# Quarter-array attention at the start, and two moved steps in later passes, of an attention and mixture-of-experts kernel

## The chip, the cores and the metric

One core of a Trainium2 chip runs the kernel. Its engines work side by side: PE (TensorE, matmul; PEld is its weight load), DVE (VectorE), ACT (ScalarE), POOL (GpSimd) and SP (SyncE), which issues the DMAs here. They meet by semaphores. The metric is the device time of one execution in microseconds (us).

## The reference

The kernel computes an attention in chunks of 64 and feeds it to a mixture of four experts, all of which see every token:

```python
scores = scale * np.matmul(q_c, k_c.transpose(0, 1, 2, 4, 3))   # q, k, v: (8, 8, 576, 64), chunks of 64
scores = scores - np.max(scores, axis=-1, keepdims=True)
attn = np.exp(scores)
attn = attn / (np.sum(attn, axis=-1, keepdims=True) + 1e-09)
out = np.matmul(attn, v_c)
...
x = np.ascontiguousarray(attn_out.transpose(0, 2, 1, 3)).reshape(B * S, H * D)   # 4608 x 512
p = domain_probs / (domain_probs.sum(-1, keepdims=True) + 1e-09)
for e in range(E):                                   # 4 experts
    h = np.maximum(x @ w1[e], 0.0)                   # 512 x 1024
    out += p[:, e:e + 1] * (h @ w2[e])               # 1024 x 512
```

## The kernel before

**Tokens and passes.** The 4608 tokens are nine sub-blocks of 512. The first is worked on in eight plain passes (n = 0 to 7), the other eight in pairs: a pair takes eight passes (8 to 15, 16 to 23 and so on to 39), each over half an expert. A product of full precision is made of three: each operand is split in a hi part (a cast to fp32r, line L432 or L915, on ACT) and a lo part (the rest, L435 or L918, on POOL or DVE), and hi x hi, lo x hi and hi x lo are added up. For a pair a pass makes seven products of sums of blocks, not eight of blocks (Strassen's way); `t1` to `t4` and `b11` to `b22` are such sums of the hidden layer or its blocks, split by `sc.hi` and `sc.lo` for halves k = 0 and 1. L740 is the one line of all these matmuls: with xh or xl as weights they are the hidden layer, with hf the output layer.

**Order.** Each engine's instructions stand in the order in which the code is written; nothing reorders them. A later pass goes through a fixed list of products (`WOVEN`), and `add(at, i, f)` puts a step f ahead of its place i. A step that stands early on its engine is done early, and all that stands behind it on this engine waits for it.

**The startup.** Before pass 0 the attention of the first 512 tokens is made, in four tiles u of 128 tokens, beside the first hidden matmuls. Per tile: `start_scores` (L1115, 64x64 matmuls), `less_max` (DVE, L307 and L309), `a_exp` (ACT, L312), `start_weights` (sums and scale on DVE, L315 to L322), `start_transpose` (PE, L1121, and a copy by ACT, L1125), `start_values` (L1135), then the hi part (L432, ACT) and the lo part (L435, DVE) of the result, which the hidden matmuls read. A tile has two chunks c, whose operands lie in partitions 0 to 63 and 64 to 127. Scores and values of a chunk use the diagonal quarters of TensorE, rows c and columns c. The results lie in PSUM banks named A0, A1, B0, B1, C0, C1, and in psa, a tile of two banks that the attention of later tiles uses as well: there `quarters()` spreads scores (L161) and values (L208) over all four quarters, with the halves of v's second chunk swapped when it is loaded, `blocks(0)` of psa for scores and `blocks(1)` for values.

**Weights of later passes.** Their hi and lo parts are made once, stored in DRAM (`slots`, L581, L597) and read back in a ring (L635). `make_next` makes one unit on ACT and POOL (L577, L578) and appends its store to `kept`; `keep_made` issues the stores waiting in `kept`. `make_before` does the same for a unit of another pass (L592, L593, stores L597). All loads and stores stand in SP's queue in order, on eight DMA lanes in turn: an issue waits for the landing of the one eight before it.

Of the kernel before, what the change touches and what calls it, by code (L numbers as in the profile page):

```python
# [31 lines left out]
def chunk_attention_moe(ctx: ExitStack, tc: tile.TileContext, qk, v, v0, dp, w1, w2, out):  # L32
# [1069 lines left out]

    def start_v(t):
        nc.sync.dma_start(out=v0s[t // GT], in_=v0[:, t : t + GT])

    def start_scores(u):

        ps = psa[:, 1] if u == 2 else bank(("A0", "A1", None, "A1")[u])
        sc[u] = ps.rearrange("p (h s) -> p h s", s=C)
        for slot in range(2 * HG):  # L1110
            t, head = cell(u, slot)
            for c in range(2):
                rows = slice(c * C, (c + 1) * C)
                q, k = (qk0[t][rows, head // HG, x, head % HG] for x in range(2))
                nc.tensor.matmul(sc[u][rows, slot], lhsT=q, rhs=k, start=True, stop=True)  # L1115

    def start_transpose(u):

        w = (bank(("B0", "B1", "B1")[u]) if u < 3 else psa[:, 0]).rearrange("p (j s) -> p j s", s=P)
        for j in range(HG):  # L1120
            nc.tensor.transpose(  # L1121
                w[:, j], es[u][:, 2 * j : 2 * j + 2].rearrange("p h s -> p (h s)"), ident
            )
        pt[u] = hpool.tile([P, HG, P], F32, name=("s2", "s4")[u % 2])
        nc.scalar.copy(out=pt[u], in_=w)  # L1125

    def start_values(u):
        av[u] = bank(("B1", "B1", "B1", "A1")[u]).rearrange("p (j s) -> p j s", s=P)
        for j in range(HG):
            t, head = cell(u, 2 * j)  # L1130
            for c in range(2):
                for half in range(2):
                    rows = slice(half * C, (half + 1) * C)
                    cols = slice(c * C, (c + 1) * C)
                    nc.tensor.matmul(  # L1135
                        av[u][rows, j, cols], lhsT=v0s[t // GT][rows, t % GT, c, head // 2],
                        rhs=pt[u][rows, j, cols], start=True, stop=True,
                    )

# [5 lines left out]
    def start_x(u):  # L1145

        if u >= GT:
            return av[u], [part[:, :, u * P : (u + 1) * P] for part in xt["plain"]]
        return (
            av[u].rearrange("p (t j) s -> p t j s", t=GT),  # L1150
            [
                part[:, 2 * u : 2 * u + 2, first].rearrange("p j (t s) -> p t j s", t=GT)
                for part in xt["plain"]
            ],
        )

# [30 lines left out]
    def load_all():  # L1187
        for g in range(2):
            for t in range(GT):
                start_load(t, slice(g, g + 1))  # L1190
        start_v(0)
        w1_quad_load(0, 0, 0)
        w1_quad_load(0, 1, 0)
        start_load(2, slice(0, 2))
        w1_quad_load(0, 0, 1)
        w1_quad_load(0, 1, 1)
        start_load(3, slice(0, 2))
        w2_load(0, (0,))
        nc.sync.dma_start(out=pr, in_=dp)

    def start_weights(u):
        es[u] = att.tile([P, 2 * HG, C], F32, name=("e", "pt")[u % 2])

        scale(es[u], sc[u], inverse_sums(sc[u], psa[:, u != 2, : 2 * HG]))

    def startup(beside):
# [14 lines left out]
        start_values(0)  # L1221
        hi_part(*start_x(0))
        a_exp(sc[1])
        w1_split(1, 0, nc.gpsimd)
        lo_part(nc.vector, *start_x(0))
        start_weights(1)
# [9 lines left out]
        start_values(1)  # L1236
        hi_part(*start_x(1))
        w1_split(1, 1, nc.gpsimd)
        a_exp(sc[2])
        start_scores(3)  # L1240
        lo_part(nc.vector, *start_x(1))
        start_weights(2)
# [26 lines left out]
        start_values(2)  # L1269
        split(nc.vector, *start_x(2))  # L1270
        o[0].part((2, 3), slice(0, dm), False, True)
# [265 lines left out]
    def first_later_pass(n, held):  # L1537
# [5 lines left out]
        def put(i, name, k):  # L1543
# [43 lines left out]
    def later_pass(n, ahead, late, held):  # L1587
# [248 lines left out]
```

## Time and profile before

| what | value |
|---|---|
| three runs | 1470.07, 1470.26, 1470.32 us |
| median | 1470.26 us |
| the profiled execution | 1471.92 us, span 1469.8 us, granted TensorE clock 0.999 |
| busy in it: PE, PEld, DVE, ACT, POOL | 1459.9, 1200.5, 1079.4, 623.2, 975.0 us |
| DMA | 348.51 MB, mean 237 GB/s |

In a row of the timeline stand the start in the span, the duration, the engine, the line, the operation, out<-in with sizes, and in brackets how long the engine was idle before it and what ended that. A row with x32 is a burst of 32 records of one line. Matmuls overlap in the array, so a burst's duration is longer by a tail than its share of the chain of waits.

### The profile page before, as it was taken

How to read it: one execution, taken by the hardware profiler on the slowest of the kernel's cores; microseconds unless marked ns; L12 is line 12 of the kernel's file. 1: busy time of each engine (PE TensorE's matmuls, PEld its weight loads, DVE VectorE, ACT ScalarE, POOL GpSimd, SP SyncE). 2: the span in 40 equal slices, each digit the busy share in tenths (PEclk: the TensorE clock that was granted, in tenths of full speed). 3: DMA queues.
4: the chain of work that ended last, by engine and by line, in shares of the span. 5: the costliest groups of instructions: out<-in, count | busy, mean ns of one | idle time of the engine just before them, and what ended most of it. 6: DMA issues, size and time to landing. Idle time of an engine off the chain costs nothing.

```text
span 1469.8 us, 23359 instructions
## 1 busy us (share of the span) xinstructions
PE 1459.9 (99%) x8556; PEld 1200.5 (82%) x8556; DVE 1079.4 (73%) x1492; ACT 623.2 (42%) x1165; POOL 975.0 (66%) x728
## 2 busy tenths in 40 slices
PE   9999999999999999999999999999999999999998
PEld 7888887888887888888888888888888888888887
DVE  5567658888887886778767977777668866666666
ACT  4556635545454434444433435444334343233332
POOL 5778888788878785555557656555557655555555
PEclk9999999999999999999999999999999999999999
DMA  8798886878779779767566788776666786666665
GB/s 308 267 332 322 309 301 227 270 239 278 237 260 306 260 233 278 243 200 232 189 209 191 231 227 271 228 242 189 202 199 202 202 252 199 197 206 194 207 189 156
DMA packets 202882, 348.51 MB, mean 237 GB/s; under 512 B 70272, under 2 KB 116112, under 8 KB 202384
## 3 DMA queue, kind: packets, MB, share of 16 engines
q1 hardware_dynamic: 202768, 347.02, 73.8%
q8 instruction: 68, 1.11, 0.3%
q14 instruction: 46, 0.38, 0.1%
HBM read 275.59 MB, written 71.38 MB: 236 GB/s over the span
## 4 chain that ended last, share of the span: by engine, by line
PE 94%; DMA 2%; POOL 2%; DVE 1%; issue 0%; ACT 0%; SPq 0%; POOLq 0%; DVEq 0%; ACTq 0%
PE A L740 49%; PE C L740 27%; PE B L740 14%; POOL hf L918 1%; PE psa L208 1%; DMA wf<-w 1%; PE psa L161 1%; PE psa L263 1%; DMA out<-acc 1%; PE B L282 0%; POOL wf L578 0%; POOL hf L435 0%; DMA wf<-in_w 0%; DMA w_sums<-acc 0%; DMA pt<-w_sums 0%
## 5 line engine op out<-in xcount | busy, mean ns | idle before, releaser
L918 POOL TENSOR_TENSOR hf<-wraw,hf 128x512 fp32r<-128x512 f32 x384 | 507.9, 1341 | 225.0 <-ACT hf L915 223.8
L740 PE MATMUL A<-hf,wf 128*128 128x512 f32 x1536 | 391.5, 390 | 1.0 <-DMA wf<-w 1.0
L740 PE MATMUL A<-xh,wf 128*128 128x512 f32 (+1 forms) x1104 | 380.7, 388 | 0.2 <-POOL wf L578 0.2
L915 ACT CAST hf<-wraw 128x512 fp32r<-128x512 f32 x384 | 233.3, 622 | 290.7 <-DVE wraw L909 99.7
L740 PEld LDWEIGHTS A<-hf,wf 128*128 128x128 f32 x1536 | 286.5, 188 | 62.9 <-DVE acc L965 1.7
L740 PEld LDWEIGHTS A<-xh,wf 128*128 128x128 f32 x1104 | 206.7, 188 | 43.6 <-POOL wf L578 0.6
L803 ACT COPY s<-A 128x512 f32<-128x512 f32 x192 | 112.8, 587 | 290.9 <-PE A L740 290.6
L740 PE MATMUL A<-xl,wf 128*128 128x512 f32 (+1 forms) x552 | 213.7, 388 | 0.0
L965 DVE TENSOR_TENSOR acc<-A,acc 128x512 f32<-128x512 f32 x232 | 157.7, 680 | 64.8 <-PE A L740 64.5
L740 PE MATMUL C<-xh,wf 128*128 128x512 f32 (+1 forms) x600 | 203.6, 386 | 0.7 <-ACT xh L432 0.7
L740 PE MATMUL C<-hf,wf 128*128 128x512 f32 x768 | 195.0, 389 | 0.7 <-POOL hf L918 0.7
L740 PEld LDWEIGHTS C<-hf,wf 128*128 128x128 f32 x768 | 144.1, 188 | 31.0 <-POOL hf L918 1.1
L740 PEld LDWEIGHTS C<-xh,wf 128*128 128x128 f32 x600 | 111.5, 188 | 24.1 <-ACT xh L432 0.8
L909 POOL TENSOR_TENSOR wf<-wraw,wf 128x512 f32<-128x512 f32 x31 | 40.1, 1292 | 130.1 <-DVE wf L903 129.2
L740 PE MATMUL B<-xh,wf 128*128 128x512 f32 (+1 forms) x376 | 125.1, 383 | 0.0
L918 POOL TENSOR_TENSOR hf<-wf,hf 128x512 fp32r<-128x512 f32 x64 | 91.1, 1424 | 48.7 <-ACT hf L915 48.7
L740 PEld LDWEIGHTS A<-xl,wf 128*128 128x128 f32 x552 | 103.5, 188 | 21.1
L965 DVE TENSOR_TENSOR acc<-C,acc 128x512 f32<-128x512 f32 x120 | 82.6, 689 | 44.3 <-PE C L740 41.3
L740 PE MATMUL C<-xl,wf 128*128 128x512 f32 (+1 forms) x300 | 114.5, 385 | 0.0
L909 DVE TENSOR_TENSOR wraw<-wf,wraw 128x512 f32<-128x512 f32 x64 | 95.7, 1495 | 6.3 <-POOL hf L918 5.2
L740 PE MATMUL B<-hf,wf 128*128 128x512 f32 x384 | 97.9, 390 | 0.0
L909 POOL TENSOR_TENSOR wraw<-wraw 128x512 f32<-128x512 f32 x63 | 92.8, 1473 | 0.0
(224 smaller groups left out, 1969.3 us busy)
## 6 DMA issues: line engine op xcount, KB each, us to landing
wf<-w SPq DMA_DIRECT2D x402, 512.0 KB, 4.3
w<-wf SPq DMA_DIRECT2D x46, 512.0 KB, 5.2
w<-hf SPq DMA_DIRECT2D x28, 512.0 KB, 7.2
qk_in<-in_qk SPq DMA_DIRECT2D x24, 512.0 KB, 6.1
w<-hf SPq DMA_DIRECT2D x42, 256.0 KB, 5.2
wf<-in_w SPq DMA_DIRECT2D x19, 512.0 KB, 6.5
ws<-p_t SPq DMA_DIRECT2D x24, 256.0 KB, 4.1
xraw<-in_w SPq DMA_DIRECT2D x24, 256.0 KB, 4.7
```

The source lines that it names most:

```text
L161: nc.tensor.matmul(s["sc"][of_half(half), c, slot], lhsT=q, rhs=k, start=True, stop=True)
L208: nc.tensor.matmul(av[of_half(slot % 2), half, head // 2], lhsT=s["v"][of_half(half), head], rhs=s["pt"][of_half(half), c, slot], start=Tr ...
L263: nc.tensor.matmul(s["sc"][of_half(half), c, slot], lhsT=q, rhs=k, start=True, stop=True)
L740: nc.tensor.matmul(out, lhsT=lhs(k, a), rhs=rhs(k, b), start=first and i == 0, stop=last and i == len(parts) - 1, skip_group_check=not (fi ...
L803: nc.scalar.copy(out=t, in_=self.a)
L909: (eng or nc.vector).tensor_tensor(out=self.values[place, k], in0=self.values[a, k], in1=self.values[b, k], op=op)
L915: nc.scalar.copy(out=self.part(name, 0)[:, k], in_=self.values[name, k])
L918: (eng or nc.gpsimd).tensor_tensor(out=self.part(name, 1)[:, k], in0=self.values[name, k], in1=self.part(name, 0)[:, k].bitcast(F32), op=A ...
L965: nc.vector.tensor_tensor(out=acc[key], in0=src, in1=acc[key], op=ALU.add)
```

## The change

- Startup, scores and values: for tiles 0 to 2 the scores go over all four quarters into `blocks(0)` of psa (before: the diagonal, into A0, A1 and a bank of psa); tile 3 stays on the diagonal in A1. The values of all four tiles go over four quarters into `blocks(1)` of psa (before: B1, for tile 3 A1). The sums of the softmax lie in psa, in columns of `blocks(1)` (tile 3: of `blocks(0)`). The transposes go to B0 and B1.
- Startup, what follows from it: hi and lo of tiles 0 and 1 are two instructions each in place of one (`start_x_hi`, `start_x_lo`), one for each half of the result. v is loaded in three DMAs, chunk 0 and the two swapped halves of chunk 1, which for tiles 0 and 1 stand behind two weight loads.
- Pass 9: hi and lo of `t4`, k = 0, move from place 0 (put there by the list `late` of `first_later_pass`) to place 9, ahead of those of k = 1 at place 10.
- Pass 14: the three `keep_made` two places behind each `make_before` are left out; the stores go with the next `keep_made` in the code.

```diff
-    def start_v(t):
-        nc.sync.dma_start(out=v0s[t // GT], in_=v0[:, t : t + GT])
+    def start_v(t, chunks=(0, 1)):
+        to, of = v0s[t // GT], v0[:, t : t + GT]
+        if 0 in chunks:
+            nc.sync.dma_start(out=to[:, :, 0], in_=of[:, :, 0])
+        if 1 in chunks:
+            for half in range(2):
+                nc.sync.dma_start(out=to[of_half(half), :, 1], in_=of[of_half(1 - half), :, 1])
+
+    def start_blocks(u):
+        for pairs in ((0, 1), (2, 3)):
+            for p in range(2):
+                for c in range(2):
+                    for j in pairs:
+                        half, group = (j & 1, 2 * c + j // 2) if u < NT - 1 else (c, j)
+                        yield c, j, p, half, group, p ^ c
 
     def start_scores(u):
-        ps = psa[:, 1] if u == 2 else bank(("A0", "A1", None, "A1")[u])
-        sc[u] = ps.rearrange("p (h s) -> p h s", s=C)
-        for slot in range(2 * HG):
-            t, head = cell(u, slot)
-            for c in range(2):
-                rows = slice(c * C, (c + 1) * C)
-                q, k = (qk0[t][rows, head // HG, x, head % HG] for x in range(2))
-                nc.tensor.matmul(sc[u][rows, slot], lhsT=q, rhs=k, start=True, stop=True)
+        if u < NT - 1:
+            sc[u] = blocks(0)
+        else:
+            sc[u] = bank("A1").rearrange("p (c h s) -> p c h s", c=2, s=C)
+        for c, j, p, half, group, place in start_blocks(u):
+            t, head = cell(u, 2 * j + p)
+            q, k = (qk0[t][of_half(c), head // HG, x, head % HG] for x in range(2))
+            nc.tensor.matmul(
+                sc[u][of_half(half), group // 2, 2 * (group % 2) + place],
+                lhsT=q, rhs=k, start=True, stop=True,
+            )
...
     def start_values(u):
-        av[u] = bank(("B1", "B1", "B1", "A1")[u]).rearrange("p (j s) -> p j s", s=P)
...
+        av[u] = blocks(1)
+        for c, j, p, half, group, place in sorted(start_blocks(u), key=lambda block: block[1]):
+            t, head = cell(u, 2 * j + p)
+            nc.tensor.matmul(
+                av[u][of_half(p), c, j], lhsT=v0s[t // GT][of_half(place), t % GT, c, head // 2],
+                rhs=pt[u][of_half(place), group, of_half(half)], start=True, stop=True,
+            )
...
-        start_v(0)
+        start_v(0, (0,))
         w1_quad_load(0, 0, 0)
         w1_quad_load(0, 1, 0)
+        start_v(0, (1,))
         start_load(2, slice(0, 2))
...
-        scale(es[u], sc[u], inverse_sums(sc[u], psa[:, u != 2, : 2 * HG]))
+        i = 0 if u == NT - 1 else HG * C
+        z = psa[:, 0, i : i + 2 * HG].rearrange("p (c j) -> p c j", c=2)
+        scale(es[u], sc[u], inverse_sums(sc[u], z))
...
-            (0, lambda: sc.hi("t4", 0)), (0, lambda: sc.lo("t4", 0)), (7, lambda: sc.sum("t4", 1)),
+            (7, lambda: sc.sum("t4", 1)),
...
-        second_half(at, ahead[0], *((9, False, (1,)) if n == n_pass + 1 else ()))
+        second_half(at, ahead[0], *((9, False) if n == n_pass + 1 else ()))
...
         if n == 2 * n_pass - 2:
             for k, i in enumerate((11, 15, 18)):
                 add(at, i, lambda k=k: make_before(k))
-                add(at, i + 2, keep_made)
```

The places where the order changes, as the built programs have it. A row names line, operation, out<-in, and the semaphores that the instruction waits for, by engine or DMA lane. First PE in the startup, from scores(1) over values(0) to the first hidden matmuls; the rows before:

```order
L1115 MATMUL A_290<-xraw 64x64 [waits DMAHW2_49]
L1115 MATMUL A_290<-xraw 64x64 x7
L1115 MATMUL A_290<-xraw 64x64 [waits DMAHW3_49]
L1115 MATMUL A_290<-xraw 64x64 x7
L1135 MATMUL B_313<-s_288,qk_in 64x64 [waits DMAHW4_49,Activation_49]
L1135 MATMUL B_313<-s_288,qk_in 64x64 x15
L740 MATMUL C_342<-xh_236,wf_310 128x256 [waits Activation_49]
L740 MATMUL C_342<-xh_236,wf_310 128x256
```

and now:

```order
L1130 MATMUL psa<-xraw 64x64 [waits DMAHW2_49]
L1130 MATMUL psa<-xraw 64x64 x7
L1130 MATMUL psa<-xraw 64x64 [waits DMAHW3_49]
L1130 MATMUL psa<-xraw 64x64 x7
L1149 MATMUL psa<-s_289,qk_in 64x64 [waits DMAHW4_49,DVE_49,Activation_49]
L1149 MATMUL psa<-s_289,qk_in 64x64 [waits DMAHW0_49]
L1149 MATMUL psa<-s_289,qk_in 64x64
L1149 MATMUL psa<-s_289,qk_in 64x64 [waits DMAHW7_49]
L1149 MATMUL psa<-s_289,qk_in 64x64 x12
L740 MATMUL C_343<-xh_238,wf_310 128x256 [waits Activation_49]
L740 MATMUL C_343<-xh_238,wf_310 128x256
```

The scores write psa where they wrote A1; values(0) write psa where they wrote B1, and their first row waits for DVE too: for the subtraction L309 of tile 1. Values(1) do so for that of tile 2, values(2) for the reciprocal of tile 3. The other two new waits are those for the two halves of v's second chunk.

DVE at the same place, from less_max(1) to the scale of tile 1 (xl is the lo part of the attention's result); before:

```order
L307 TENSOR_REDUCE m_307<-A_290 128x8 [waits PE_49]
L309 TENSOR_TENSOR A_290<-A_290,m_307 128x512 [waits DVE_49]
L435 TENSOR_TENSOR xl_237<-B_313,xh_236 128x2x2x128 [waits Activation_49]
L315 TENSOR_REDUCE psa<-A_290 128x8 [waits Activation_49]
L316 TENSOR_SCALAR psa<-psa 128x8 [waits DVE_49]
L318 RECIPROCAL z_339<-psa 128x8 [waits DVE_49]
L322 TENSOR_TENSOR pt<-A_290,z_339 128x512 [waits DVE_49]
```

and now:

```order
L307 TENSOR_REDUCE m_307<-psa 128x8 [waits PE_49]
L309 TENSOR_TENSOR psa<-psa,m_307 128x2x256 [waits DVE_49]
L435 TENSOR_TENSOR xl_239<-psa,xh_238 128x2x2x64 [waits PE_49,Activation_49]
L435 TENSOR_TENSOR xl_239<-psa,xh_238 128x2x2x64
L315 TENSOR_REDUCE psa<-psa 128x8 [waits DVE_49]
L316 TENSOR_SCALAR psa<-psa 128x8 [waits DVE_49]
L318 RECIPROCAL z_340<-psa 128x8 [waits DVE_49]
L322 TENSOR_TENSOR pt<-psa,z_340 128x512 [waits DVE_49]
```

The lo part has become two instructions. Its wait on ACT was for the hi part; it is now for the exponential of tile 1, which stands behind the hi part on ACT, as that lies in the same banks.

POOL in pass 9 (hf_2683 before and hf_2795 now are t4; hf_2677 and hf_2680 are t1; L578 makes ring weights), before:

```order
L918 TENSOR_TENSOR hf_2616<-wraw,hf_2616 128x512
L918 TENSOR_TENSOR hf_2677<-wraw,hf_2677 128x512
L918 TENSOR_TENSOR hf_2683<-wraw,hf_2683 128x512
L918 TENSOR_TENSOR hf_2677<-wraw,hf_2677 128x512
L918 TENSOR_TENSOR hf_2707<-wraw,hf_2707 128x512 x2
L918 TENSOR_TENSOR hf_2723<-wf_2579,hf_2723 128x512
L578 TENSOR_TENSOR wf_2727<-xraw,wf_2727 128x2x256
L918 TENSOR_TENSOR hf_2723<-wf_2579,hf_2723 128x512
L578 TENSOR_TENSOR wf_2779<-xraw,wf_2779 128x2x256
L918 TENSOR_TENSOR hf_2683<-wraw,hf_2683 128x512
L578 TENSOR_TENSOR wf_2816<-xraw,wf_2816 128x2x256
```

and now:

```order
L918 TENSOR_TENSOR hf_2619<-wraw,hf_2619 128x512
L918 TENSOR_TENSOR hf_2680<-wraw,hf_2680 128x512 x2
L918 TENSOR_TENSOR hf_2707<-wraw,hf_2707 128x512 x2
L918 TENSOR_TENSOR hf_2723<-wf_2582,hf_2723 128x512
L578 TENSOR_TENSOR wf_2727<-xraw,wf_2727 128x2x256
L918 TENSOR_TENSOR hf_2723<-wf_2582,hf_2723 128x512
L578 TENSOR_TENSOR wf_2779<-xraw,wf_2779 128x2x256
L918 TENSOR_TENSOR hf_2795<-wraw,hf_2795 128x512 x2
L578 TENSOR_TENSOR wf_2819<-xraw,wf_2819 128x2x256
```

The first of the two pieces of t4 has moved down to the second, and what stood between the two (a piece of t1, three of other sums and blocks, two of L578) has moved up by one.

SP at the end of pass 14 (w_0_6_187 is the unit that `make_next` has made, w_0_0_195 and w_1_0_188 are loads for pass 15, w_1_1_203 and w_1_2_204 units of `make_before`), before:

```order
L597 DMA w_1_1_203<-pt 256x1x256 [waits DMAHW1_49,Pool_49]
L581 DMA w_0_6_187<-wf_5004 128x1024 [waits DMAHW2_49,Pool_49]
L635 DMA wf_5014<-w_0_0_195 128x1024 [waits DMAHW3_49,PE_49]
L635 DMA wf_5027<-w_1_0_188 128x1024 [waits DMAHW4_49,PE_49]
L597 DMA w_1_2_204<-xraw 256x1x256 [waits DMAHW5_49,Activation_49]
L597 DMA w_1_2_204<-v_in 256x1x256 [waits DMAHW6_49,Pool_49]
```

and now:

```order
L597 DMA w_1_1_203<-pt 256x1x256 [waits DMAHW5_49,Pool_49]
L635 DMA wf_5016<-w_0_0_195 128x1024 [waits DMAHW7_49,DMAHW6_49,PE_49]
L635 DMA wf_5029<-w_1_0_188 128x1024 [waits PE_49]
L581 DMA w_0_6_187<-wf_5007 128x1024 [waits DMAHW0_49,Pool_49]
L597 DMA w_1_2_204<-xraw 256x1x256 [waits DMAHW1_49,Activation_49]
L597 DMA w_1_2_204<-v_in 256x1x256 [waits DMAHW2_49,Pool_49]
```

The store of w_0_6 stands behind the two loads now. It waits for POOL; the loads wait for PE, which must have read the tiles that they fill.

More of the change, by code (lines that the diff above doesn't have):

```diff
@@ L1101, in start_load @@
         )
-    def start_v(t):
-        nc.sync.dma_start(out=v0s[t // GT], in_=v0[:, t : t + GT])
-    def start_scores(u):
-        ps = psa[:, 1] if u == 2 else bank(("A0", "A1", None, "A1")[u])
-        sc[u] = ps.rearrange("p (h s) -> p h s", s=C)
-        for slot in range(2 * HG):
-            t, head = cell(u, slot)
-            for c in range(2):
-                rows = slice(c * C, (c + 1) * C)
-                q, k = (qk0[t][rows, head // HG, x, head % HG] for x in range(2))
-                nc.tensor.matmul(sc[u][rows, slot], lhsT=q, rhs=k, start=True, stop=True)
+    def start_v(t, chunks=(0, 1)):
[12 more added lines that the diff above has]
+                        yield c, j, p, half, group, p ^ c
+    def start_scores(u):
+        if u < NT - 1:
[9 more added lines that the diff above has]
+            )
     def start_transpose(u):
-        w = (bank(("B0", "B1", "B1")[u]) if u < 3 else psa[:, 0]).rearrange("p (j s) -> p j s", s=P)
+        w = bank("B1" if u else "B0").rearrange("p (j s) -> p j s", s=P)
         for j in range(HG):
             nc.tensor.transpose(
-                w[:, j], es[u][:, 2 * j : 2 * j + 2].rearrange("p h s -> p (h s)"), ident
+                w[:, j], es[u][:, j // 2, 2 * (j % 2) : 2 * (j % 2) + 2].rearrange("p h s -> p (h s)"), ident
             )
@@ L1127, in start_values @@
     def start_values(u):
-        av[u] = bank(("B1", "B1", "B1", "A1")[u]).rearrange("p (j s) -> p j s", s=P)
[L1129 to L1138, printed above, removed]
+        av[u] = blocks(1)
[5 more added lines that the diff above has]
+            )
     first = slice(0, GT * P)
@@ L1145, in start_x, with start_x_hi, start_x_lo @@
     def start_x(u):
[L1147 to L1152, printed above, removed]
-                for part in xt["plain"]
-            ],
-        )
+        for t in range(GT) if u < GT else (u,):
+            j, k = (slice(2 * t, 2 * t + 2), slice(2 * u, 2 * u + 2)) if u < GT else (slice(0, HG),) * 2
+            yield av[u][:, :, j], [
+                part[:, k, t * P : (t + 1) * P].rearrange("p j (c s) -> p c j s", c=2)
+                for part in xt["plain"]
+            ]
+    def start_x_hi(u):
+        for x in start_x(u):
+            hi_part(*x)
+    def start_x_lo(u):
+        for x in start_x(u):
+            lo_part(nc.vector, *x)
     def start_hidden(u, fs, terms):
@@ L1201, in start_weights @@
     def start_weights(u):
-        es[u] = att.tile([P, 2 * HG, C], F32, name=("e", "pt")[u % 2])
-        scale(es[u], sc[u], inverse_sums(sc[u], psa[:, u != 2, : 2 * HG]))
+        es[u] = att.tile([P, 2, HG, C], F32, name=("e", "pt")[u % 2])
+        i = 0 if u == NT - 1 else HG * C
+        z = psa[:, 0, i : i + 2 * HG].rearrange("p (c j) -> p c j", c=2)
+        scale(es[u], sc[u], inverse_sums(sc[u], z))
     def startup(beside):
@@ L1221, in startup @@
         start_values(0)
-        hi_part(*start_x(0))
+        start_x_hi(0)
         a_exp(sc[1])
         w1_split(1, 0, nc.gpsimd)
-        lo_part(nc.vector, *start_x(0))
+        start_x_lo(0)
         start_weights(1)
@@ L1236, in startup @@
         start_values(1)
-        hi_part(*start_x(1))
+        start_x_hi(1)
         w1_split(1, 1, nc.gpsimd)
@@ L1240, in startup @@
         start_scores(3)
-        lo_part(nc.vector, *start_x(1))
+        start_x_lo(1)
         start_weights(2)
@@ L1269, in startup @@
         start_values(2)
-        split(nc.vector, *start_x(2))
+        start_x_hi(2)
+        start_x_lo(2)
         o[0].part((2, 3), slice(0, dm), False, True)
@@ L1275, in startup @@
         start_values(3)
-        split(nc.vector, *start_x(3))
+        start_x_hi(3)
+        start_x_lo(3)
         o[1].part((2, 3), slice(0, dm), False, True)
@@ L1699, in later_pass, with second_half @@
         return (sc, left), late, ()
-    def second_half(at, sc, t4=6, sum4=True, ks=range(2)):
+    def second_half(at, sc, t4=6, sum4=True):
         add(at, 0, lambda: sc.sum("t2", 1))
@@ L1708, in second_half @@
             add(at, 4, lambda: sc.sum("t4", 1, nc.gpsimd))
-        for k in ks:
+        for k in range(2):
             add(at, t4 + k, lambda k=k: sc.hi("t4", k), lambda k=k: sc.lo("t4", k))
```

## The prediction

> **What bounds the kernel.** I read the page first, then the waits of PE (TensorE), then the timeline of the places that the page cannot resolve: the first 33 us, and the ends of passes 9 and 14. Here is the page's busy time by engine, and all that PE waited for others from 100 us on (total, times, longest):
>
> ```profile
> PE 1459.9 (99%) x8556; PEld 1200.5 (82%) x8556; DVE 1079.4 (73%) x1492; ACT 623.2 (42%) x1165; POOL 975.0 (66%) x728
> PE A L740 <- DMA wf<-w: 1.0, 1, 1.0
> PE C L740 <- POOL hf L918: 0.7, 1, 0.7
> PE A L740 <- POOL wf L578: 0.2, 1, 0.2
> ```
>
> PE is busy for 1459.9 of 1469.8 us, so 9.9 us is all that hiding waits can bring. The edits of passes 9 and 14 aim at the three rows, 1.9 us together. And where PE has no idle time left, nothing swallows a delay: a microsecond lost in the startup is lost at the end.
>
> **Startup: what gets shorter.** Timeline (start, duration, engine, line, operation, out<-in; in brackets the idle time before and what ended it). L1115 are the scores, L1121 the transposes, L1135 the values; L307 and L309 less_max, L315 to L322 sums and scale, all on DVE (VectorE); L740 the hidden layer. The last row but two is a stretch of the table by windows, with DMA share and GB/s at its end:
>
> ```profile
> 3.86 1.97 PE L1115 MATMUL A<-xraw 64*64 64x64 f32 x32
> 10.04 0.63 PE L1121 MATMUL B<-ident,e 128*128 128x128 f32 x4 [1.39 <-DVE e L322]
> 10.60 1.15 PE L1115 MATMUL A<-xraw 64*64 64x64 f32 x32
> 11.58 1.10 PE L1135 MATMUL B<-s,qk_in 64*64 64x64 f32 x32
> 11.79 0.69 DVE L307 TENSOR_REDUCE m<-A 128x8 f32<-128x512 f32 x1 [1.90 <-PE A L1115]
> 12.52 0.70 DVE L309 TENSOR_TENSOR A<-A,m 128x512 f32<-128x512 f32 x1
> 13.36 1.22 PE L740 MATMUL C<-xh,wf 128*128 128x256 f32 x8 [0.69 <-ACT xh L432]
> 13.95 0.69 DVE L315 TENSOR_REDUCE psa<-A 128x8 f32<-128x512 f32 x1
> 14.42 0.64 PE L740 MATMUL C<-xl,wf 128*128 128x256 f32 x4
> 15.13 0.69 DVE L322 TENSOR_TENSOR pt<-A,z 128x512 f32<-128x512 f32 x1
> 16.35 0.60 PE L1121 MATMUL B<-ident,pt 128*128 128x128 f32 x4
> 17.87 1.10 PE L1135 MATMUL B<-s,qk_in 64*64 64x64 f32 x32
> 3.00:10.00 7.00, 5.65 (x45) 2.83 (x43) 3.16 (x6) 0.58 (x1) 0.00 (x0) 1.00 0.96 315
> 55.44 0.69 PE L208 MATMUL psa<-pt,v_in 64*64 64x64 f32 x32
> 55.96 0.70 PE L161 MATMUL psa<-qk_in 64*64 64x64 f32 x32
> ```
>
> The last two rows are values and scores as later passes do them, in four quarters: 0.70 us for 32 records, where the diagonal takes 1.15. So two scores and four values each save about 0.45. The first scores run slow (1.97); at 0.70/1.15 of that they take 1.20 and save 0.77. Softmax, transposes and the next scores hang on them: transposes(0) move from 10.04 to 9.27, and scores(1) run from 9.83 to 10.53. If nothing else changed, that would be 0.77 + 6 x 0.45, about 3.5 us.
>
> **Startup: the new waits.** Before, scores and values lay in different banks, and values(0) ran from 11.58, beside the softmax of tile 1. Now both lie in the two banks of psa, and in the instruction order values(u) carries a wait on DVE: for the subtraction (L309) of tile u+1 in the same banks. The lo part on DVE, likewise, now waits for the exponential of tile u+1 on ACT (ScalarE). Work that overlapped comes one after the other. Link by link, with these durations:
> - less_max(1) starts 0.04 behind scores(1), at 10.57, takes 0.69 and 0.70 and ends at 12.00. values(0) run from 12.12 to 12.81; before, they ended at 12.68. What scores(0) and scores(1) won is gone.
> - hi(0) becomes two casts of 128x256. The nearest row (ACT L747, next fence) has 0.66 for two; hidden(0) starts at 13.55 for 13.36: +0.19.
> - exp(1) (0.59, next fence) follows on ACT to 14.11, then lo(0), two pieces with 0.75 (DVE L748, next fence), from 14.15 to 14.90. The hidden matmuls that need it stood at 14.42: +0.53. Sums and scale of tile 1 took 13.95 to 15.82, 1.87; from 14.93 they end at 16.80, and transposes(1) start at 16.92 for 16.35: +0.57.
> - scores(2) run from 17.45 to 18.15, less_max(2) ends at 19.62, values(1) run from 19.74 to 20.43; before, they ended at 18.97: +1.46.
>
> The rows for tiles 2 and 3 (the one without a line's operation is from the chain of waits):
>
> ```profile
> 19.01 0.59 ACT L432 CAST xh<-B 128x512 fp32r<-128x512 f32 x1 [0.92 <-PE B L1135]
> 20.02 0.59 ACT L312 ACTIVATE psa<-psa 128x512 f32<-128x512 f32 x1
> 21.56 0.66 ACT L747 ACTIVATE hf<-C 128x256 fp32r<-128x256 f32 x2
> 21.82 0.69 DVE L322 TENSOR_TENSOR e<-psa,z 128x512 f32<-128x512 f32 x1
> 22.43 0.75 DVE L748 SCALAR_TENSOR_TENSOR hf<-C,hf 128x256 fp32r<-128x256 f32 x2
> 22.66 0.63 PE L1121 MATMUL B<-ident,e 128*128 128x128 f32 x4 [0.17 <-DVE e L322]
> 26.10 0.21 DVE L318 RECIPROCAL z<-psa 128x8 f32<-128x8 f32 x1
> 26.23 2.28 PE C L740 x9
> 29.17 0.68 DVE L435 TENSOR_TENSOR xl<-B,xh 128x512 fp32r<-128x512 f32 x1
> 29.67 1.15 PE L1135 MATMUL A<-s,ws 64*64 64x64 f32 x32
> ```
>
> - hi(1) starts at 20.45. exp(2) stood 1.01 behind the start of hi(1); with 0.07 for the split cast it runs from 21.53 to 22.12, lo(1) to 22.91, and 1.87 of sums and scale, with the gap ahead of them, to 24.81 for 22.51: +2.30. transposes(2) start at 24.95 for 22.66.
> - values(2) now wait for the reciprocal of tile 3, whose sums lie in psa as well. From the end of scale(2), 22.51, to that of this reciprocal, 26.31, DVE took 3.80; now 24.81 + 3.80 = 28.61. values(2) run from 28.73 to 29.35. Before, the next work on the chain began at 26.23: +3.1.
> - Behind them stands the same PE work as before, 26.23 to 29.67. So values(3) start at 32.79, take 0.70 for 1.15, and end at 33.5 for 30.82. Their wait for lo(2) ends earlier: DVE took 26.10 to 29.85 from reciprocal to lo(2), now 28.40 to 32.15.
>
> **Startup: +2.7 us.** Outer bounds: -3.5 if every new wait is hidden, +3.2 if values(3) win nothing. Each link is a row, so I stay with +2.7. The least sure is the wait of values(2): PE came from transposes(2) to them in 2.42, now by 27.37, and sits idle for 1.36; half of that hidden leaves +2.0. The three DMAs for v in place of one move the same bytes: with chunk 1 behind two weight loads, 2.1 MB have to land, at 315 GB/s and from about 3 us between 10 and 11, ahead of 12.1. Were that cover gone, values(0) would be late by the same amount.
>
> The Trainium skill, PSUM — Partial Sum Buffer, section "PSUM bank collisions raise a hardware error", has it that two engines are kept apart by bank and quadrant, not by address, which is how shared banks come to cost waits; a guard by address would leave the gains alone, the bound of -3.5. The instruction order has the guard; its price no run shows yet.
>
> **Pass 9.** PE and POOL (GpSimd) near its end:
>
> ```profile
> 228.93 10.35 POOL L918 TENSOR_TENSOR hf<-wraw,hf 128x512 fp32r<-128x512 f32 x7
> 236.64 0.74 PE L740 MATMUL C<-hf,wf 128*128 128x512 f32 x2 [0.70 <-POOL hf L918]
> 242.19 0.73 PE L740 MATMUL A<-xh,wf 128*128 128x512 f32 x2 [0.19 <-POOL wf L578]
> 245.05 1.29 POOL L918 TENSOR_TENSOR hf<-wraw,hf 128x512 fp32r<-128x512 f32 x1
> 247.31 1.63 PE L740 MATMUL A<-hf,wf 128*128 128x512 f32 x6
> ```
>
> POOL works without a gap, 10.35/7 = 1.48 us a piece, and PE waits for it twice, 0.70 and 0.19. One hi (ACT) and one lo (POOL) of t4 go from ahead of both waits to place 9: 1.3 to 1.5 us less on POOL ahead of them, more than 0.89. What is late next is t4 itself: its last lo ended at 246.34 and is used at 247.31, and with the moved piece in front it keeps that time, less the 0.89 that PE arrives earlier: 0.1 us of slack. Bounds: -0.89, and +0.5 if t4 is late by most of a piece. I take -0.9, as POOL has the same work in all.
>
> **Pass 14.** SP (the queue that issues DMAs), and from the chain of waits the load and PE's work behind it; the last row is the table by windows:
>
> ```profile
> 457.71 1.36 SPq L597 DMA_DIRECT2D w<-pt  x1
> 461.33 0.33 SPq L581 DMA_DIRECT2D w<-wf  x1
> 461.75 1.17 SPq L635 DMA_DIRECT2D wf<-w  x2
> 462.22 8.83 DMA wf<-w
> 471.18 3.01 PE A L740 x12
> 455.00:485.00 30.00, 28.97 (x128) 23.66 (x127) 21.50 (x26) 12.01 (x21) 25.68 (x19) 1.00 1.00 352
> ```
>
> SP stands from 459.07 to 461.33 at the store L581, whose data POOL had still to make, and two loads are queued behind it; the second lands at 471.05 and PE waits 1.03 for it. Now both stand ahead of the store and can go from 459.1. The DMA engines are full (share 1.00, 352 GB/s), so what counts is the bytes that go behind: 512 KB, or 1.49 us. The load lands at 469.6, ahead of 470.15. What is late next is the store, which no one reads in this pass. Bounds: 0, if something else holds the loads, and -1.03; I take -1.0.
>
> **Sum.** +2.7 - 0.9 - 1.0 = +0.8 us. The profiled execution took 1471.92 (span 1469.8), 1.66 above the median of 1470.26; I put the difference on the median: 1471.1.
>
> **Rivals.**
> - The gain is real: the new waits are hidden for the greater part. Startup between -3.5 and 0, at -1.7 a total of -3.6: 1466.7. For it speaks each shorter step; against it, that values(0) cannot start before 12.0 if they wait for a subtraction that needs scores(1). Chance 0.14.
> - Slower: PE loses its pace. The first scores took 1.97 for 32 records, the next 1.15. PE will now sit idle ahead of values(0), (1) and (2) for 1.6, 1.6 and 1.4 us. If one such gap brings the slow pace back, the hidden matmuls behind it, 3.0 us from 13.36 to 16.35, cost 0.71 more each: +2.1, in all +2.9, 1473.2; two gaps give 1475.3. One gap decides it. Against it: after 1.39 us of idling ahead of 10.04, scores(1) ran at 1.15. Chance 0.10.
> - The edits of passes 9 and 14 don't do what they say, startup as worked out: +2.7 and up to +0.5, 1473.0 to 1473.5. For it: the full DMA engines and t4's slack of 0.1. Chance 0.08.
>
> The Trainium skill, TensorE: Matmul & The Clock Gate, Part 1, says that the clock falls back after an idle window of about 3.4 us; by that rule none of these gaps is long enough, and the sum stays as it is.
>
> **How the numbers follow.** My own case has 0.68: from +2.0 - 1.9 to +3.2 - 0.4, 1470.3 to 1473.1. The range adds most of the gain's case below and half of the slow pace above: 1467.4 to 1473.9. A difference under 0.2%, 2.9 us, is about what a measurement cannot tell from none, so faster ends at 1467.3 and slower begins at 1473.2. Faster gets 0.10 of the gain's 0.14, and 0.04 for changes in the long passes that I don't see; slower gets 0.08 of the slow pace, 0.05 of the failed edits and 0.04 of my own case.
>
> **What would show it.** Scores(1) and all values at 0.70 us; PE idle ahead of values(0), (1) and (2) with DVE L309 or L318 as what ended it, 1.4 to 1.6 us each; values(3) ending near 33.5; no wait near 236.6 and 471.2. If values(0) start before 11.9, the wait is not what I take it for. If the twelve hidden matmuls after values(0) take over 2.5 us, PE lost its pace. A new wait of PE for t4 or for a later load would undo a pass's part.

## The result and the profile after

The changed kernel takes 1473.33 us (median of 21 runs, 1471.33 to 1474.13), the kernel before 1470.91 (21 runs, 1469.69 to 1473.58). The ratio is 1.0015, with a 95% interval of 1.0008 to 1.0021: slower by some 2.2 us, which is inside the 0.2% named above. The profiled execution of the changed kernel took 1473.44, its span is 1471.6.

How the loss and the gains lie along the span can be read from marks that both traces have: the first attention scores after the startup (L161), the last values before pass 9 (L208), the first scores behind pass 9, the last values before pass 14, and the last DVE copy. Timeline rows (start, duration, engine, line), before:

```profile
40.83 0.74 PE L161 MATMUL psa<-qk_in 64*64 64x64 f32 x32
160.90 0.69 PE L208 MATMUL psa<-pt,v_in 64*64 64x64 f32 x32
248.87 0.74 PE L161 MATMUL psa<-qk_in 64*64 64x64 f32 x32
447.47 0.69 PE L208 MATMUL psa<-pt,v_in 64*64 64x64 f32 x32
1465.86 0.42 DVE L1734 COPY s<-B 128x256 f32<-128x256 f32 x1 [0.53 <-PE B L1765]
```

and after:

```profile
45.66 0.74 PE L161 MATMUL psa<-qk_in 64*64 64x64 f32 x32
165.67 0.69 PE L208 MATMUL psa<-pt,v_in 64*64 64x64 f32 x32
252.22 0.74 PE L161 MATMUL psa<-qk_in 64*64 64x64 f32 x32
450.79 0.69 PE L208 MATMUL psa<-pt,v_in 64*64 64x64 f32 x32
1467.86 0.42 DVE L1756 COPY s<-B 128x256 f32<-128x256 f32 x1 [0.53 <-PE B L1787]
```

The shifts are +4.83, +4.77, +3.35, +3.32 and +2.00. So the startup lost 4.8 us, the stretch with pass 9 won 1.4, the one with pass 14 won 1.3, and between them the shift stayed within 0.06. From 36 us on the table of PE's waits has one row left, against four of before:

```profile
PE B L1787 <- DVE acc L1779: 0.3, 1, 0.3
```

The startup after (L1130 scores, L1139 transposes, L1149 values):

```profile
3.86 1.14 PE L1130 MATMUL psa<-xraw 64*64 64x64 f32 x32
9.22 0.63 PE L1139 MATMUL B<-ident,e 128*128 128x128 f32 x4 [1.90 <-DVE e L322]
9.78 0.69 PE L1130 MATMUL psa<-xraw 64*64 64x64 f32 x32
12.07 1.13 PE L1149 MATMUL psa<-s,qk_in 64*64 64x64 f32 x32 [1.59 <-issue]
13.96 2.07 PE L740 MATMUL C<-xh,wf 128*128 128x256 f32 x8 [0.76 <-ACT xh L432]
15.83 1.05 PE L740 MATMUL C<-xl,wf 128*128 128x256 f32 x4
19.04 0.60 PE L1139 MATMUL B<-ident,pt 128*128 128x128 f32 x4
21.91 0.69 PE L1149 MATMUL psa<-s,qk_in 64*64 64x64 f32 x32 [1.64 <-DVE psa L309]
30.90 0.69 PE L1149 MATMUL psa<-s,ws 64*64 64x64 f32 x32 [1.26 <-issue]
34.97 0.69 PE L1149 MATMUL psa<-s,ws 64*64 64x64 f32 x32
```

The scores became as short as expected, and PE waits ahead of values(0), (1) and (2) for 1.59, 1.64 and 1.26. But the rows from values(0) to 18.7 run slowly: 2.07 for eight hidden matmuls where before had 1.22, 1.13 for values(0) where values(1) take 0.69. The table by windows (length, busy of the engines, then PE's granted clock, DMA share, GB/s) shows why, after:

```profile
7.00:10.40 3.40, 1.50 (x38) 0.97 (x36) 1.77 (x4) 0.68 (x3) 0.00 (x0) 1.00 1.09 294
10.40:13.96 3.56, 1.21 (x39) 0.97 (x32) 1.39 (x2) 1.26 (x5) 1.26 (x1) 0.71 1.07 380
13.96:19.00 5.04, 5.04 (x24) 5.04 (x25) 2.52 (x6) 1.08 (x2) 1.28 (x1) 0.53 1.07 326
19.00:24.00 5.00, 3.36 (x106) 3.01 (x105) 1.39 (x2) 2.45 (x6) 1.36 (x2) 1.00 0.53 167
```

The two figures 0.71 and 0.53 are means: by the trace's clock records the granted clock is 0.50 from 11.92 to 18.75 us and 1.00 on either side. In the profile of before no such fall lies in the startup.

### The profile page after: what moved, and what is told of

Same layout as the page of the kernel before. It is cut to its first block, busy times and chain, and to the rows that moved or that the text cites. A ratio compares the mean times of both kernels' runs of the same rounds, so it can differ in the third digit from the quotient of the medians.

```text
span 1471.6 us, 23370 instructions
## 1 busy us (share of the span) xinstructions
PE 1458.2 (99%) x8556; PEld 1199.9 (82%) x8556; DVE 1078.6 (73%) x1494; ACT 623.2 (42%) x1167; POOL 975.6 (66%) x728
## 4 chain that ended last, share of the span: by engine, by line
PE 95%; POOL 2%; issue 1%; DVE 1%; ACT 1%; DMA 1%; POOLq 0%; SPq 0%; ACTq 0%
PE A L740 50%; PE C L740 27%; PE B L740 14%; POOL hf L435 1%; PE psa L208 1%; POOL wf L435 1%; PE psa L263 1%; PE psa L161 1%; PE B L282 0%; DMA w<-xl 0%; ACT hf L432 0%; PE psa L1149 0%; PE C L1204 0%; DMA w<-hf 0%; PE B L1139 0%
```

## The experiments

Each is compared with the kernel before on the same chip; its median there is given with it.

**The two parts of the change.** `passes` is the kernel before with the lines of passes 9 and 14 only:

```diff
-            (0, lambda: sc.hi("t4", 0)), (0, lambda: sc.lo("t4", 0)), (7, lambda: sc.sum("t4", 1)),
+            (7, lambda: sc.sum("t4", 1)),
-        second_half(at, ahead[0], *((9, False, (1,)) if n == n_pass + 1 else ()))
+        second_half(at, ahead[0], *((9, False) if n == n_pass + 1 else ()))
-                add(at, i + 2, keep_made)
```

> The kernel before with only the edits of passes 9 and 14. My theory: the three waits go, each costing more than its idle time, since the last matmul before it runs out its 0.39 us instead of handing over after 0.23 and the next pair starts slower; from the traces 1.42 in pass 9 and 1.33 in pass 14, 2.75 us together, so 1468.2 against 1470.9 for the kernel before. The rival (the 1.9 us of idle time that the waits' table shows is all): 1469.0. The waits' table from 100 us on should be empty but for the one at the end (0.3).

1469.55 for 1471.21, ratio 0.9988 (0.9979 to 0.9997): 1.7 us faster. In the profile all three waits are gone, and the last copy (DVE) stands at 1463.51, 2.35 earlier than in the profile of before. The median says less than this, and less than the 2.75 of my theory; it is nearest to the rival's 1.9. Why shows below.

`startup` is the other part: the changed kernel with these lines as they were.

> The kernel before with only the startup of the changed kernel. My theory: values(3) end 4.8 us later than before, 35.7 for 30.8, and nothing gives that back: 1475.7 against 1470.9. If parts of the 4.8 belong to the pace of PE and not to the waits, and the pace changes from run to run, the times spread by some 2 us. The rival (the startup is what the prediction's sum had, +2.7): 1473.6. The first later waits, 0.7, 0.2 and 1.0, are back.

1474.94 for 1471.21, ratio 1.0026 (1.0016 to 1.0036): 3.7 us slower, between the two theories. With the 1.7 of `passes` that gives +2.0, the 2.2 measured of both. So the parts add up within the noise, and the startup is where the change loses.

**Is it the clock?** `warm` gives PE more of the matmuls that only fill its idle time:

```diff
-WAITS = {"loads": 6, "softmax": 10}
+WAITS = {"loads": 6, "softmax": 17}
...
         start_scores(1)
+        keep_warm(6)
         less_max(sc[1])
```

> The changed kernel with more filler matmuls on PE (17 for 10 ahead of the first transposes, and 6 new ones between scores(1) and values(0)), which only fill its idle time. Theory A (part of the loss is PE's clock, which the profile grants at 0.53 to 0.71 from 10.4 to 19 us): granted clock 1.00 there, values(0) in 0.7 for 1.13, twelve hidden matmuls in 1.7 for 2.93, transposes(1) at about 17.3 for 19.04, and 1.7 us faster than the changed kernel: 1471.6 for 1473.3. Theory B (the slow stretch comes from something else, the DMA load at a share of 1.07 or the banks): the same 1473.3 and the same durations.

1471.92 for 1471.21, ratio 1.0004 (0.9995 to 1.0013), against 1.0015 of the changed kernel: by the medians, 1.4 to 1.7 us of the loss are the clock. Its windows:

```profile
10.40:14.00 3.60, 2.65 (x63) 1.50 (x56) 1.39 (x2) 1.74 (x5) 1.26 (x1) 1.00 1.07 365
14.00:19.00 5.00, 4.25 (x60) 3.74 (x59) 3.02 (x7) 1.98 (x4) 1.28 (x1) 1.00 1.08 335
```

and its timeline:

```profile
9.52 0.60 PE L1139 MATMUL B<-ident,e 128*128 128x128 f32 x4
12.34 0.69 PE L1149 MATMUL psa<-s,qk_in 64*64 64x64 f32 x32 [0.20 <-issue]
13.79 1.22 PE L740 MATMUL C<-xh,wf 128*128 128x256 f32 x8 [0.76 <-ACT xh L432]
17.21 0.60 PE L1139 MATMUL B<-ident,pt 128*128 128x128 f32 x4
20.07 0.70 PE L1149 MATMUL psa<-s,qk_in 64*64 64x64 f32 x32 [1.64 <-DVE psa L309]
25.32 0.63 PE L1139 MATMUL B<-ident,e 128*128 128x128 f32 x4 [0.31 <-DVE e L322]
29.07 0.70 PE L1149 MATMUL psa<-s,ws 64*64 64x64 f32 x32 [1.25 <-issue]
33.16 0.69 PE L1149 MATMUL psa<-s,ws 64*64 64x64 f32 x32
```

Clock 1.00, values(0) in 0.69, with the same DMA share and the same shared banks: theory B is out. Values(1) and (2) wait as they do after (1.64 and 1.25); ahead of values(0) the filler takes the place of the idle time, and they start no earlier. Transposes(1) stand 1.83 earlier than after, close to the 1.7 expected. The longer filler itself delays transposes(0) by 0.3.

**Are the waits those for the shared banks?** `v0banks` is the changed kernel with values(0) in banks of their own:

```diff
-        av[u] = blocks(1)
+        if u == 0:
+            av[u] = [bank(name)[:, : HG * C].rearrange("p (j k) -> p j k", k=C) for name in ("A1", "B1")]
+            to = lambda c: av[u][c]
+        else:
+            av[u] = blocks(1)
+            to = lambda c: av[u][:, c]
...
-                av[u][of_half(p), c, j], lhsT=v0s[t // GT][of_half(place), t % GT, c, head // 2],
+                to(c)[of_half(p), j], lhsT=v0s[t // GT][of_half(place), t % GT, c, head // 2],
...
```

> The changed kernel, but values(0) go to two banks of their own (A1 for chunk 0, B1 for chunk 1), still in four quarters; hi and lo of tile 0 are made by chunk. Theory A (values(0) wait for the subtraction because they share psa's banks with scores(1)): they start when the copied transposes and v are there, 10.5 to 11.2 for 12.07, lo(0) no longer waits for the exponential of tile 1, and with one gap less PE keeps its clock: transposes(1) at about 16.0 for 19.04, 2.5 to 3 us faster than the changed kernel, 1470.6. values(1) still sit idle for 1.6. Theory B (it is v's second chunk that comes late, or the four quarters themselves): values(0) start at 12.0 as before and the time stays at 1473.3.

```profile
10.31 0.33 PE L1154 MATMUL A<-s,qk_in 64*64 64x64 f32 x2
11.04 0.37 PE L1154 MATMUL B<-s,qk_in 64*64 64x64 f32 x1 [0.40 <-DMA qk_in<-in_v]
17.98 0.60 PE L1139 MATMUL B<-ident,pt 128*128 128x128 f32 x4
20.84 0.69 PE L1154 MATMUL psa<-s,qk_in 64*64 64x64 f32 x32 [1.64 <-DVE psa L309]
```

Values(0) start at 10.31 for 12.07, so it was the shared banks that held them, though the profile of the changed kernel puts that wait down to "issue". They then wait 0.40 for v's second chunk: it lands at about 11.0, which the 12.0 of the changed kernel covers. Values(1), still in psa, sit idle for 1.64 as before. What I had not expected: the clock fell in this profile too (0.57 from 10.4 to 14 us), and transposes(1) came at 17.98, not 16.0. The median is 1471.41 for 1471.12, ratio 1.0000 (0.9991 to 1.0009); the runs lie from 1469.95 to 1473.46, five of eleven below 1470.7. The eight runs whose granted clock is 0.999 or 1.000 have a median of 1470.58, the 1470.6 that theory A expected with the clock held.

`z3` is `warm` with the sums of tile 3 in SBUF:

```diff
+        if u == NT - 1:
+            z = small.tile([P, 2, HG], F32, name="zsum")
...
```

> The changed kernel with the added filler (so that the clock holds), and with the softmax sums of tile 3 in SBUF instead of psa. Theory A (values(2) wait for the reciprocal of tile 3 because its sums lie in their bank): the idle time of 1.25 us ahead of values(2) at 29.07 goes; values(3) then wait for lo(2) on DVE at about 32.2 and give some of it back: 0.8 to 1.2 us faster than with the filler alone, 1470.9 for 1471.9. Theory B (something else ends that wait): values(2) still start at 29.07.

```profile
27.38 0.69 PE L1149 MATMUL psa<-s,ws 64*64 64x64 f32 x32
32.75 0.69 PE L1149 MATMUL psa<-s,ws 64*64 64x64 f32 x32 [1.06 <-DVE xl L435]
31.93 0.68 DVE L435 TENSOR_TENSOR xl<-psa,xh 128x512 fp32r<-128x512 f32 x1
```

The wait ahead of values(2) is gone, so it was the reciprocal's. But values(3) wait 1.06 for lo(2) instead, and lo(2) stands on DVE behind softmax and normalising. From transposes(0) (9.15 here, 9.52 in `warm`) to values(3) it is 23.60 against 23.64. The time, 1471.33 for 1471.12, ratio 1.0001 (0.9993 to 1.0010), can't be told from `warm`. Expected were 0.8 to 1.2 us: a wait removed at one place came back at the next, with DVE as the bound.

**What lowers the clock?** `gap5` is `passes` with less filler ahead of the first transposes:

```diff
-WAITS = {"loads": 6, "softmax": 10}
+WAITS = {"loads": 6, "softmax": 5}
```

> The kernel with only the edits of passes 9 and 14 (1469.55), and 5 filler matmuls for 10 ahead of the first transposes, so that PE sits idle for some 2.8 us there instead of 1.4 to 1.6; all that follows is as before. Theory A (the clock falls with the share of time that PE works in a stretch of some us, so that two gaps of 1.9 and 1.6 did it in the changed kernel, and this one does it too): granted clock under 1.00 somewhere from 10 to 16 us, hidden(0) slower, 1 to 2 us longer. Theory B (only an idle stretch of about 3.4 us, the figure of the Trainium skill, TensorE: Matmul & The Clock Gate, Part 1, lowers it): granted clock 1.00 in all stretches, 1469.6.

The transposes of `gap5` with their idle time in the timeline:

```profile
9.27 0.63 PE L1121 MATMUL B<-ident,e 128*128 128x128 f32 x4 [3.03 <-DVE e L322]
```

and its windows:

```profile
7.00:10.40 3.40, 1.13 (x23) 1.00 (x25) 1.77 (x4) 0.68 (x2) 0.00 (x0) 1.00 1.03 364
10.40:14.00 3.60, 2.92 (x55) 2.73 (x52) 2.03 (x4) 1.89 (x5) 1.27 (x1) 0.56 1.07 383
14.00:19.00 5.00, 5.00 (x35) 4.83 (x36) 1.73 (x5) 0.48 (x2) 1.27 (x1) 0.63 1.03 405
```

An idle stretch of 3.03, with none of the change's banks and waits, lowers the clock to a mean of 0.56. The times spread from 1468.96 to 1473.99 (median 1471.14 for 1471.12): in some executions it falls and in some it doesn't. And it can fall in the startup of before. The run of `pass9` (below) that was profiled shows it, behind an idle stretch of 1.95 alone; timeline, then windows:

```profile
9.25 0.63 PE L1121 MATMUL B<-ident,e 128*128 128x128 f32 x4 [1.95 <-DVE e L322]
```

```profile
10.40:14.00 3.60, 2.92 (x55) 2.73 (x52) 2.03 (x4) 1.87 (x5) 1.26 (x1) 0.55 1.07 383
```

This execution took 1472.07; the other nine of the same kernel took 1469.35 to 1469.79. So the fall cost about 2.4 us there. In the profile of `pass14` an idle stretch of 1.94 at the same place, 0.8 later in time, left the clock at 1.00:

```profile
10.04 0.63 PE L1121 MATMUL B<-ident,e 128*128 128x128 f32 x4 [1.94 <-DVE e L322]
```

Length alone does not decide, then. The clock records kept in the traces show what does go with the fall. They begin where PE first gets its full clock, and that time differs from execution to execution. It shows in the length of scores(0), here in `pass9`, with the same diagonal matmuls that took 1.97 in the profile of before:

```profile
3.86 1.18 PE L1115 MATMUL A<-xraw 64*64 64x64 f32 x32
```

Count stretches of 3.41 us from that time on. In each of the five traces with a fall, the clock falls at the end of the second stretch and stays at 0.50 for the next two, 6.83 us. The busy share is that of PE in this second stretch, by the table by windows:

| trace | full clock from, us | idle time ahead of transposes(0) | second stretch, us | PE busy in it | clock at its end |
|---|---|---|---|---|---|
| after | 5.10 | 1.90 | 8.51 to 11.92 | 0.37 | falls |
| `startup` | 4.43 | 1.97 | 7.84 to 11.26 | 0.37 | falls |
| `v0banks` | 4.05 | 1.96 | 7.46 to 10.88 | 0.46 | falls |
| `gap5` | 4.00 | 3.03 | 7.42 to 10.83 | 0.46 | falls |
| `pass9` | 3.96 | 1.95 | 7.38 to 10.79 | 0.45 | falls |
| `best` (below) | 3.99 | 1.96 | 7.41 to 10.82 | 0.54 | holds |
| `pass14` (below) | 5.73 | 1.94 | 9.14 to 12.56 | 0.74 | holds |
| `passes` | 6.52 | 1.59 | 9.93 to 13.34 | 0.77 | holds |
| before | 6.92 | 1.39 | 10.33 to 13.74 | 0.80 | holds |

In the 13 traces of this case, counted in this way up to 1450 us, these five are the only stretches in which PE was busy for less than half of the time; the next lowest has 0.52, and the clock held. So it is the share of work in a stretch of 3.41 us that goes with the fall, and where the stretches lie differs between executions of one kernel. This is read off the traces afterwards; no run sets the place of the stretches. The Trainium skill, TensorE: Matmul & The Clock Gate, Part 1, has the clock fall after an idle window of about 3.4 us and speaks of a free-running window; the traces agree with such a window and not with the need for 3.4 us of rest: a window in which PE worked for 0.37 to 0.46 of the time was enough.

The timed runs show the same. A fall of 6.83 us to half the clock takes 0.0023 off the mean granted clock, which each run lists. Of the 21 runs of the changed kernel 13 have 0.997 or 0.998 (median 1473.44) and eight have 0.999 or 1.000 (median 1472.47); of the kernel before, on the three chips of the experiments, 7 of 83 have 0.997; of `gap5` 7 of 10 have 0.998 or less; of `warm`, `z3` and the three faster kernels below none of 48. So the fall is in most executions of the changed kernel, and without it that kernel is still slower than the kernel before. The two groups of its runs lie only 1.0 apart. One reason is in the traces: the falls came with an early full clock (3.96 to 5.10 us), which can shorten scores(0), as in `pass9`.

**The passes one by one.** `pass9` and `pass14` are the kernel before with the one or the other of the two edits.

> The kernel before with the edit of pass 9 alone. Theory (each of the two waits costs its idle time and the tail of the matmul ahead of it, and the first pair behind it is slow): the attention of pass 10 begins 1.4 us earlier, 247.5 for 248.87, though the waits' table loses only 0.9; the wait for the load at the end of pass 14 stays. 1.0 to 1.4 us faster than the kernel before. The rival (t4 comes late in return): a new wait of PE near 246, and 0.4 us or less.

> The kernel before with the edit of pass 14 alone. Theory: SP issues both loads at about 459 instead of 461.8 and 462.2, the wait of 1.0 us for the load goes, 1.0 to 1.3 us faster than the kernel before; the two waits of pass 9 stay. The rival (other loads of the full DMA engines come later in return): a new wait for a load between 470 and 490, no gain.

`pass9`: 1469.62 for 1470.83, ratio 0.9992 (0.9983 to 1.0001, which just reaches none), 1.2 us; no wait for t4 appears. `pass14`: 1471.03 for 1470.83, ratio 1.0002 (0.9993 to 1.0011), no gain that can be measured (the interval reaches from 1.0 us faster to 1.6 slower), although in its profile SP issues both loads 2.3 us earlier and no wait for a load is left:

```profile
459.50 1.83 SPq L635 DMA_DIRECT2D wf<-w  x2
```

The table of waits shows what there was to win. The same wait, unedited, in the profiles of `pass9` and then of `startup`:

```profile
PE A L740 <- DMA wf<-w: 0.4, 1, 0.4
```

```profile
PE A L740 <- DMA wf<-w: 0.7, 2, 0.5
```

It is 0.4 and 0.7 there, where the profile of before has 1.0: the DMA engines are full at this place (share 1.00 in the prediction's windows), and the wait varies from profile to profile. The profiled execution of before took 1471.92, 1.0 above the median of its 21 runs. A wait read from that one execution can be worth less in the median. The traces speak for some gain: from the last values before pass 14 to the last copy it is 1016.89 to 1017.46 us in the ten profiles with the edit and 1017.73 to 1018.39 in the three without. Whether it is worth nothing or a whole microsecond the timed runs don't settle.

**The gain without the waits.** `scores4` is `passes`, and of the startup only the scores in four quarters, with the values where they were and v in one DMA. Against the lines of the changed kernel:

```diff
-                        yield c, j, p, half, group, p ^ c
+                        yield c, j, p, half, group, p
...
-        av[u] = blocks(1)
+        av[u] = bank(("B1", "B1", "B1", "A1")[u]).rearrange("p (j s) -> p j s", s=P)
...
-                av[u][of_half(p), c, j], lhsT=v0s[t // GT][of_half(place), t % GT, c, head // 2],
+                av[u][of_half(p), j, of_half(c)], lhsT=v0s[t // GT][of_half(p), t % GT, c, head // 2],
```

> The edits of passes 9 and 14, and of the startup's change only the scores: in four quarters, in psa, while values stay on the diagonal in B1 and A1 with v as it was. No bank is shared, so no new wait stands in the order. Theory A (the loss is the shared banks' waits): scores(0) save 0.8, scores(1) and (2) 0.45 each, so the startup ends 1.3 to 1.7 us earlier than before, and with 2.75 of the passes the time is 1466.6. Theory B (four quarters in the startup lose by themselves, as PE gets more idle time and its clock drops): granted clock under 1.00 between 10 and 19 us and a startup that is no shorter, 1468.2 or more.

1468.74 for 1471.21, ratio 0.9982 (0.9973 to 0.9991). The first L161 stands at 39.79 for 40.83: the startup is 1.04 shorter, less than the 1.3 to 1.7 expected, with the clock at 1.00. Against `passes`, measured beside it, the median is 0.8 shorter. No shared bank, no wait, a gain.

`best` adds the values of tiles 2 and 3 in four quarters in psa (with `p ^ c` for these tiles, and their second chunk of v swapped) and the sums of tile 3 in SBUF; `best2` also moves `norm_probs()` behind lo(2).

> The version with scores in four quarters and values(0), (1) on the diagonal (1468.74), and now values(2) and (3) in four quarters in psa, where no scores lie any more at that time, with the sums of tile 3 in SBUF. Theory A (four quarters gain their 0.45 us wherever no shared bank puts a wait on the path): values(2) in 0.70 for 1.20 without a wait, values(3) the same but up to 0.3 late for lo(2): 0.6 to 0.9 us faster, 1468.0. Theory B (PE isn't the bound there, DVE's chain is): values(3) end no earlier, 1468.7.

> The version with scores and the last two tiles' values in four quarters (1467.45), with the normalising of the probabilities on DVE moved behind lo(2). Theory A (DVE's order ahead of lo(2), 2.3 us of that normalising, makes the 0.80 us that values(3) wait): the wait goes, values(3) start at 27.8 for 28.56, 0.7 us faster, 1466.7. Theory B (the first use of the probabilities, the scaling of the output block on DVE, then comes late and holds a bank): values(3) start early, but PE waits later; the time stays at 1467.4.

`best`: 1467.45 for 1471.12, ratio 0.9972 (0.9960 to 0.9983). `best2`: 1467.18 for 1470.83, ratio 0.9975 (0.9966 to 0.9985). The timeline has the values of tiles 2 and 3 in `best`:

```profile
23.64 0.69 PE L1152 MATMUL psa<-s,ws 64*64 64x64 f32 x32
28.56 0.69 PE L1152 MATMUL psa<-s,ws 64*64 64x64 f32 x32 [0.80 <-DVE xl L435]
```

and those of tile 3 with the first wait behind them in `best2`:

```profile
28.07 0.70 PE L1152 MATMUL psa<-s,ws 64*64 64x64 f32 x32
30.87 0.39 PE L740 MATMUL B<-xl,wf 128*128 128x256 f32 x1 [0.41 <-DVE xl L435]
```

In `best` values(3) wait for lo(2). In `best2` that wait is gone, and PE waits 0.41 for lo(3) instead. Both versions beat the kernel before by some 3.7 us and can't be told apart. That is theory B of `best2`, with another wait than the one it named.

## Why the prediction was right, and where it was off

- **The total.** +0.8 was forecast, +2.2 measured (1473.33, or 1473.1 by the ratio on the median before). It lies in the range and, as forecast, within 0.2%. As a change it also lies in the prediction's own case (+0.1 to +2.8), as a time at or above the end of that case (1473.1), since 21 runs put the kernel before 0.65 higher than the three that the prediction started from. But the startup in it, +3.7 by the medians, is outside the +2.0 to +3.2 of that case: the total came by way of the slow pace, whose rival stood at +2.9 and 1473.2. In so far as the number fits the own case, that is luck.
- **Startup, the waits: right.** Each link is found again in `warm`, where the clock holds, if its later transposes(0) are taken off (9.52 for 9.27, 0.25): values(0) 12.34 (forecast 12.12), hidden(0) 13.79 (13.55), transposes(1) 17.21 (16.92), values(1) 20.07 (19.74), transposes(2) 25.32 (24.95), values(2) 29.07 (28.73), values(3) 33.16 (32.79). Less the 0.25 none is off by more than 0.12. By the medians the startup of `warm` costs 1471.92 - 1469.55 (`passes`, measured beside it), +2.4 for the +2.7 forecast, with the 0.25 of the filler in it. The wait of values(2), called the least sure, measured 1.25 to 1.26 for 1.36. One link was right by luck: the 0.77 saved on scores(0) came from a profile in which PE had its full clock only from 6.92, and the profile after is of the same kind there (1.14 for 1.97). Where the full clock comes at about 4 us, the diagonal takes 1.18 to 1.20 (`pass9`, `gap5`) and the quarters 0.83 to 0.92 (`best`, `v0banks`), which saves 0.3. The prediction took the slow pace as fixed.
- **Startup, the sum of +2.7: too small,** 4.8 in the trace and 3.7 in the median. The step that failed is the argument against the second rival, the loss of pace: that 1.39 us of idling ahead of 10.04 had left the clock alone. The changed kernel idles 1.90 there, as scores(0) and the filler behind them end earlier, and 1.59 soon after. The rival's mechanism and its place were right, and its price of +2.1 was near (1.83 between the traces of after and `warm`, 2.13 with the later start of `warm`; 1.4 to 1.7 in the median); its chance of 0.10 was too low. It stands beside the waits and not in their place, and in part follows from them: of the 2.16 us that PE idles in the 3.41 us ahead of the fall, 1.44 are the wait of values(0). But the waits are not needed for it: the clock also fell in `v0banks`, without that wait, and in `pass9`, with the startup of before.
- **Pass 9: mis-sized.** -0.9 forecast, -1.42 in the trace, -1.2 in the median. In these rows a wait costs more than its idle time: PE counts as busy while the last matmul ahead of it runs out its 0.39 us, where the next would have followed after 0.23, and the pair behind it takes 0.74 for 0.62. t4, with its 0.1 us of slack, was not late.
- **Pass 14: mis-sized.** The loads do go earlier and the wait is gone, as forecast, and the trace shows -1.3. But the timed runs of `pass14` show no gain, with an interval that still admits the -1.0. The term was taken from one execution whose wait was longer than in others (1.0 for 0.4 and 0.7).
- **The gain rival, 1466.7,** fell with the waits. `best` shows what a gain of that size takes, 1467.45: scores in quarters, and values in quarters only for the tiles where no shared bank is waited for. Four quarters for all the values without a shared bank were not run.
- **The rival of the failed edits, 1473.0 to 1473.5,** has the measured number as well, but not the mechanism: `passes` wins 1.7 of the 1.9 that was put on passes 9 and 14.

The Trainium skill, PSUM — Partial Sum Buffer, section "PSUM bank collisions raise a hardware error", was weighed in the prediction; the rows agree that the guard by bank has a price here, 1.59, 1.64 and 1.26 us of idle time.

## What to carry to other kernels

Before two results are put in the same PSUM banks, ask which engine still works on the other one: a shorter burst of 0.45 us was paid with waits of 1.3 to 1.6. Where a chain of engines sets the pace, removing one wait moves it to the next link (values(2) to values(3), lo(2) to lo(3)), so follow the chain to its end before a gain is booked. And look at the granted clock when a change opens idle time on TensorE, in every timed run and not only in the profiled one: 13 filler matmuls in idle time were worth about 1.5 us.

## What the hardware showed that I had not expected

- The granted clock fell to 0.50 for 6.83 us after a stretch of 3.41 us in which PE was busy for 0.37 to 0.46 of the time, in all five traces that have such a stretch and in none of the other eight. Where the stretches lie differs between executions of the same kernel, so the fall is in some and not in others: in one of ten runs of `pass9`, where it cost 2.4 us, and in seven of ten of `gap5`.
- A short stall can cost more than its idle time in the profile: 0.89 us of waits in pass 9 were 1.42 us of progress between the profiles of before and after. Between the marks on both sides of pass 9, the ten profiles without the two waits take 86.47 to 87.40 us and the three with them 87.87 to 88.02, so the gain differs by execution, from 0.5 to 1.6.
